# A gated linear-attention kernel with a two-layer head: products and casts moved from GpSimd to VectorE, and a new step table

## The chip, the cores and the metric

The kernel runs on one core of one Trainium2 chip. The metric is the device time of one execution in microseconds (us). Each time below is the median of several executions on the chip. A run that is over 1.5% above the fastest of the same kernel is labelled slow and is left out of the ratios. The chip is not the same for all groups of runs; the kernel before ran beside each group, so kernels of different groups are compared by their ratio to it.

A core has a matrix engine (TensorE, PE in the profile; its weight loads are PEld), a vector engine (VectorE, DVE), an activation engine (ScalarE, ACT), a general engine (GpSimd, POOL) and a small one that here only issues DMAs (SyncE, SP). "SPq" is SyncE's instruction queue. Times in a trace are from the start of the span of that execution.

## The reference

The first half is an mLSTM cell: batch 4, 8 heads, 768 steps, head size 40, in fp32. The second half is a two-layer head with a squareplus between the layers.

```python
for t in range(S):                       # per batch row and head
    m_new  = max(f_gate[t] + m, i_gate[t])
    f_stab = exp(f_gate[t] + m - m_new);  i_stab = exp(i_gate[t] - m_new);  m = m_new
    C = f_stab * C + i_stab * outer(v[t], k[t])
    n = f_stab * n + i_stab * k[t]
    y[t] = sigmoid(o_gate[t]) * (C @ q[t]) / max(abs(n @ q[t]), 1.0)
x = y  as [B*S, H*D]                     # 3072 x 320
h = x @ w_in                             # 320 -> 2048
out = (0.5 * (h + sqrt(h*h + 4))) @ w_out   # 2048 -> 320, fp32
```

The kernel computes the recurrence in a short form for tiles of 128 steps (it checks on the chip that the gates allow this).

## The kernel before

There are 12 blocks: 4 batch rows with 3 pairs of 128-step tiles. For each block, q is cast to bf16 (`qb`), transposed (`qT`), multiplied with the row's state (`np`; for the first tile of a row there are also scores of q and k, `sp`), scaled (`y`), gated (`xt`), and transposed again (`xT`). Then come four groups of hidden units (`hp`, 12 matmuls each; Square and Sqrt on ScalarE; `gt` on VectorE) and the second matmuls (`op`). All engines have hand-made instruction orders. A slot is one hidden group, a step is half a slot, and a table says at which step each piece of attention work of a later block is put into the stream.

```python
STEPS = {   # per block: pr = cast of q, q_ = transpose of q, n0/n1 = scores+y+gate of a tile, x = transpose of x
    ...
    4: dict(pr=16, q_=18, n0=20, n1=23, x=26),
    5: dict(pr=19, k_=19, q_=22, s0=25, s1=26, n0=28, n1=30, x=34),
    ...
}
QDMA = (2, 3, 5, 6, 7, 8, 9, 10, 11)   # blocks whose q is transposed by a DMA
XDMA = (3, 4, 5, 7, 8, 9, 10, 11)      # the same for x
ROWS = (11, 23, 41)                    # steps at which the next batch row's loads are issued
...
        def crossbar(out, in_):
            nc.sync.dma_start(out=out, in_=in_, transpose=True)      # issued by SyncE
...
        def s_num(blk, t, tag, peng=nc.gpsimd):
            ...                                                      # np on TensorE; den, y1 on VectorE
            for lo, o in ((0, xt[blk % 2][:, t, 0:DM]), (DM - 64, xt[blk % 2][:, t, DM:])):
                peng.tensor_tensor(out=o, in0=y[:, lo:DM], in1=s[:, lo:DM], op=ALU.mult)   # the gate product
...
        def load_row(b):                                             # all issued by GpSimd
            chunk(kf, "kf", k, b, nc.gpsimd)                         # 80 KB
            chunk(vf, "vf", v, b, nc.gpsimd)                         # 80 KB
            later(ql, "ql", q, b, 1, NTL, nc.gpsimd)                 # 800 KB
            later(ol, "ol", o_gate, b, 1, NTL, nc.gpsimd)            # 800 KB
            chunk(q0, "q0", q, b, nc.gpsimd)                         # 160 KB
            chunk(o0, "o0", o_gate, b, nc.gpsimd)                    # 160 KB
...
        for n, hs in enumerate(ROWS):
            pre.setdefault(hs, []).append(lambda n=n: load_row(n + 1))
...
                at(pre, 2 * slot)          # casts and loads of this step, on GpSimd
                at(plan, 2 * slot)         # transposes, scores, gates of this step
```

GpSimd works through one list in which gate products, casts and the issue of loads stand in order, and a product in that list waits for VectorE's `y`. SyncE has a second list, in which transposing DMAs and output stores stand in order, and a store waits for its eviction.

Of the kernel before, what the change touches and what calls it, by code (L numbers as in the profile page):

```python
# [8 lines left out]
BF = mybir.dt.bfloat16  # L9
I32 = mybir.dt.int32  # L10
AF = mybir.ActivationFunctionType
ALU = mybir.AluOpType
# [3 lines left out]


STEPS = {
    1: dict(pr=None, q_=1, n0=3, n1=3, x=4),
    2: dict(pr=9, k_=1, q_=11, s0=12, s1=13, n0=13, n1=13, x=15),  # L20
    3: dict(pr=13, g=14, q_=14, n0=16, n1=17, x=18),
    4: dict(pr=16, q_=18, n0=20, n1=23, x=26),
    5: dict(pr=19, k_=19, q_=22, s0=25, s1=26, n0=28, n1=30, x=34),
    6: dict(pr=28, g=33, q_=30, n0=36, n1=34, x=39),
    7: dict(pr=33, q_=38, n0=42, n1=44, x=52),
    8: dict(pr=42, k_=43, q_=45, s0=50, s1=52, n0=53, n1=55, x=60),
    9: dict(pr=52, g=58, q_=53, n0=60, n1=59, x=65),
    10: dict(pr=62, q_=63, n0=68, n1=70, x=71),
    11: dict(pr=68, k_=68, q_=68, s0=73, s1=77, n0=79, n1=80, x=85),
}  # L30
SIGM = (15, 30, 58)
EARLY = (2, 3, 7, 8, 13, 14, 15, 16, 17, 18, 23, 24, 25, 31, 34, 39, 40, 42)
SECOND = (0, 0, 0, 0, 0, 2, 0, 1, 1, 2, 1, 1, 1, 1, 1, 1, 0, 2, 0, 1, 0, 1, 1, 1, 1, 1, 2, 1, 1, 2, 1, 1, 0, 2, 1, 1, 0, 1, 1, 0, 2, 0, 2, 1)
QT = (1, 2, 9, 10, 11)
XT = (3, 5, 7, 11)
OUT = (0, 2, 3, 13, 17, 19, 20, 21, 22)
ALONE = (4, 5, 6, 7, 8, 9, 12, 13, 14, 15, 18, 19, 24, 25, 26, 27, 30, 31, 34, 35, 38, 39, 40, 41, 42, 43)
QDMA = (2, 3, 5, 6, 7, 8, 9, 10, 11)
XDMA = (3, 4, 5, 7, 8, 9, 10, 11)
CLEAR = 8  # L40
ROWS = (11, 23, 41)
FLAGS = (56, 67, 75, 82)


def general_path(tc, q, k, v, i_gate, f_gate, o_gate, out, w_in, w_in3, w_out, ident):
# [144 lines left out]
def kernel(  # L190
# [12 lines left out]
    nc = tc.nc  # L203
    B, H, S, D = q.shape
# [8 lines left out]
    G3 = 3  # L213
# [4 lines left out]
    NU = NF // UF  # L218

    const = ctx.enter_context(tc.tile_pool(name="const", bufs=1))  # L220
    short = ExitStack()
    res = short.enter_context(tc.tile_pool(name="res", bufs=1))
    work = short.enter_context(tc.tile_pool(name="work", bufs=2))
# [13 lines left out]
    with tc.manual_schedule():  # L237
# [80 lines left out]
        for i in range(2):  # L318
            for m in (qb[i][:, 0], qb[i][:, 1]):
# [7 lines left out]
                                     op0=ALU.add, op1=ALU.bypass)  # L327
        nc.vector.tensor_tensor(out=nb[:, 0, :], in0=F[:, 0:T], in1=fi[:, 1, 0:T], op=ALU.subtract)
        nc.vector.tensor_tensor_scan(out=nb[:, 1, :], data0=nb[:, 0, :], data1=nb[:, 0, :], initial=1e30,
                                     op0=ALU.min, op1=ALU.bypass)  # L330
# [7 lines left out]
        state = {}  # L338
# [34 lines left out]
        def qcast(blk, eng, ts=(0, 1)):  # L373
            b = blk // 3
            for t in ts:
                tt = PAIRS[blk % 3][t]
                src = q0[b] if tt == 0 else tile_of(ql, b, tt)
                for o, i in zip(padded(qb[blk % 2][:, t]), heads(src)):
                    eng.tensor_copy(out=o, in_=i)  # L379
# [62 lines left out]
            nc.vector.tensor_tensor(out=state[b, "scm"][:, half * 3:half * 3 + len(hs), :], in0=sp,  # L442
                                    in1=caus.unsqueeze(1).to_broadcast([128, len(hs), 128]), op=ALU.mult)

        def s_num(blk, t, tag, peng=nc.gpsimd):
            b, tt = blk // 3, PAIRS[blk % 3][t]
            np_ = psum([128, H, D + 1], FP, tag, "np")
            if tt == 0:
                for n, h in enumerate((0, 2, 3, 5, 6)):
                    if n % 2:  # L450
                        o, r = np_[:, h:h + 1, :], state[b, "vw"][:, h:h + 1, :]
                    else:
                        o, r = np_[:, h:h + 2, :], vpb[b % 2][:, n // 2, :, :]
                    nc.tensor.matmul(out=o, lhsT=state[b, "scm"][:, n, :], rhs=r, start=True, stop=True)
            else:
                for g in range(G3):
                    n = min(3, H - 3 * g)
                    nc.tensor.matmul(out=np_[:, 3 * g:3 * g + n, :], lhsT=state[blk, "qT"][:, t, g, :],  # L458
                                     rhs=state[b, "gm"][:, 3 * g:3 * g + n, :], start=True, stop=True)
            den = work.tile([128, H, 1], FP, tag="den", name="den", bufs=3)  # L460
            dn = np_[:, :, D:D + 1]
            nc.vector.tensor_reduce(out=den, in_=dn, axis=AX.X, op=ALU.max, apply_absolute_value=True)  # L462
            y1 = work.tile([128, H, D], FP, tag="y1", name="y1", bufs=3)
            if tt == 0:
                nc.vector.tensor_tensor(out=den, in0=den, in1=wE[:, 1, b * H:(b + 1) * H].unsqueeze(2), op=ALU.max)
                nc.vector.reciprocal(out=den, in_=den)
                nc.vector.tensor_tensor(out=y1, in0=np_[:, :, 0:D], in1=den.to_broadcast([128, H, D]), op=ALU.mult)
            else:

                nc.vector.reciprocal(out=den, in_=den)  # L470
                nc.vector.scalar_tensor_tensor(out=y1, in0=den.to_broadcast([128, H, D]), scalar=1.0, in1=np_[:, :, 0:D],  # L471
                                               op0=ALU.min, op1=ALU.mult)
            y, s = (a.rearrange("p h d -> p (h d)") for a in (y1, state[b, "sig"][:, tt]))
            for lo, o in ((0, xt[blk % 2][:, t, 0:DM]), (DM - 64, xt[blk % 2][:, t, DM:])):
                peng.tensor_tensor(out=o, in0=y[:, lo:DM], in1=s[:, lo:DM], op=ALU.mult)  # L475

        def s_x(blk, tag):
            if blk in XDMA:
                xT = work.tile([128, 2, G3, 128], BF, tag="xT", name="xT", bufs=3)
                crossbar(xT.rearrange("p t g n -> p (t g) n"), xt[blk % 2].rearrange("p t n -> p (t n)"))  # L480
                state[blk, "xT"] = xT
                return
            xp = psum([128, 2, G3, 128], BF, tag, "xp")
            for t in range(2):
                for g in range(G3):
                    nc.tensor.transpose(xp[:, t, g, :], xt[blk % 2][:, t, g * 128:(g + 1) * 128], ident)
            xT = work.tile([128, 2, G3, 128], BF, tag="xT", name="xT", bufs=3)
            evacuate(XT, blk, xT, xp)
            state[blk, "xT"] = xT
# [3 lines left out]
        def idle(n):  # L493

            for _ in range(n):
                nc.tensor.matmul(out=warm[:, 0:128], lhsT=ident, rhs=ident, start=True, stop=True)  # L496
# [11 lines left out]

        for o, i in zip(padded(qb[0][:, 1]), heads(tile_of(ql, 0, 2))):
            nc.scalar.activation(out=o, in_=i, func=AF.Copy)  # L510
        idle(8)
        tp = [psum([128, 384], BF, "hp", "tp") for t in range(2)]
        np_ = psum([128, 2 * H, 64], FP, "hp", "np")
        qT = work.tile([128, 2, G3, 128], BF, tag="qT", name="qT")
        for t in range(2):
            for g in range(G3):
                nc.tensor.transpose(tp[t][:, g * 128:(g + 1) * 128], qb[0][:, t, g, :], ident)
        nc.vector.tensor_copy(out=qT[:, 0], in_=tp[0].rearrange("p (g n) -> p g n", g=G3))
        nc.scalar.activation(out=qT[:, 1], in_=tp[1].rearrange("p (g n) -> p g n", g=G3), func=AF.Copy)
        sigm(0, 1, 3)  # L520
        idle(4)
        for t in range(2):
            for g in range(G3):
                n = min(3, H - 3 * g)
                nc.tensor.matmul(out=np_[:, t * H + 3 * g:t * H + 3 * g + n, 0:D + 1], lhsT=qT[:, t, g, :], rhs=state[0, "gm"][:, 3 * g:3 * g + n, :],
                                 start=True, stop=True)
        den = const.tile([128, 2 * H, 1], FP, name="den0")
        y1 = const.tile([128, 2, H, D], FP, name="y0")
# [3 lines left out]
                                       in1=np_[:, :, 0:D], op0=ALU.min, op1=ALU.mult)  # L532
# [65 lines left out]
        def put_pre(hs, blk):  # L598
            b = blk // 3
            todo = pre.setdefault(hs, [])  # L600
            if blk % 3 == 2 and b:
                todo.append(lambda: khcast(b, nc.gpsimd))
            if blk % 3 == 0:
                todo.append(lambda: kcast(b, nc.gpsimd))
                todo.append(lambda: vcast(b, nc.gpsimd))
            todo.append(lambda: qcast(blk, nc.gpsimd))

        def put_block(blk, pr, q_, n0, n1, x, g=None, k_=None, s0=None, s1=None):
            b = blk // 3
# [18 lines left out]
        for n, hs in enumerate(ROWS):  # L628
            pre.setdefault(hs, []).append(lambda n=n: load_row(n + 1))
        for b, hs in enumerate(SIGM):  # L630
            put(hs, sigm, b + 1, 0, NTL)
        early.update(EARLY)
        for hs, f in zip(FLAGS, (flag1, flag2, flag3, flag4)):
            put(hs, f)
# [75 lines left out]
        def unit(blk, u):  # L710

            hp = hps.pop((blk, u))
            t1 = moe.tile([128, UF, 256], FP, tag="t1", name="t1")
            nc.scalar.activation(out=t1, in_=hp, func=AF.Square, scale=0.5)  # L714
            nc.scalar.activation(out=t1, in_=t1, func=AF.Sqrt, bias=1.0)  # L715
            return lambda: nc.vector.scalar_tensor_tensor(out=gts[blk][:, u * UF:(u + 1) * UF, :], in0=hp, scalar=0.5, in1=t1,  # L716
                                                          op0=ALU.mult, op1=ALU.add)

        todo = list(range(NBLK * NU - NU))
# [22 lines left out]
        blk = NBLK - 1  # L742
# [60 lines left out]
```

## Time and profile before

| | before |
|---|---|
| time, median of 3 runs | 155.05 us (154.83 to 156.91) |
| span of the profiled execution | 152.4 us |
| mean granted TensorE clock in it | 0.995 |
| busy us of PE, DVE, ACT, POOL | 132.8, 100.8, 121.7, 77.4 |

### The profile page before, as it was taken

The numbers are of one execution on the slowest core, as the hardware profiler recorded it, in microseconds if no ns is written. First come the engines' busy times: TensorE is split into PE (matmuls) and PEld (weight loads), VectorE is DVE, ScalarE is ACT, GpSimd is POOL, SyncE is SP. The second block draws the span as 40 slices with busy tenths as digits, with TensorE's granted clock in tenths as the row PEclk, the third lists the DMA queues.
The fourth block names the chain that finished last, engine by engine and source line by source line (L and its number), as shares of the span: only waits on it lengthen the run. The fifth ranks groups of instructions, "written<-read, shape, count | busy, mean of one in ns | idle before, by whom it ended". The sixth has DMA issues, their size and how long they took to land.

```text
span 152.4 us, 3186 instructions
## 1 busy us (share of the span) xinstructions
PE 132.8 (87%) x1185; PEld 93.3 (61%) x1185; DVE 100.8 (66%) x190; ACT 121.7 (80%) x130; POOL 77.4 (51%) x168
## 2 busy tenths in 40 slices
PE   6697679747999995899999899899999999999970
PEld 5684446435578673667775677666677676666740
DVE  4764556666778678388787689775799794765410
ACT  3648959938999779999997568999979989699610
POOL 7998889975363997337969014448022050000000
PEclk9999999999999999999999999999999999999997
DMA  2999999999037699503799150132333103101111
GB/s 49 253 239 197 191 211 210 282 301 124 34 78 120 138 342 227 143 28 84 225 308 162 68 149 4 43 95 54 101 103 84 60 31 95 43 6 41 71 65 49
DMA packets 29140, 19.45 MB, mean 128 GB/s; under 512 B 20752, under 2 KB 27200, under 8 KB 29120
## 3 DMA queue, kind: packets, MB, share of 16 engines
q0 software_dynamic: 5824, 10.49, 29.6%
q1 hardware_dynamic: 22240, 8.55, 26.3%
q10 hardware_dynamic: 1056, 0.16, 0.7%
q8 instruction: 10, 0.16, 0.4%
q14 instruction: 10, 0.08, 0.2%
HBM read 13.96 MB, written 3.93 MB: 117 GB/s over the span
## 4 chain that ended last, share of the span: by engine, by line
PE 52%; DVE 16%; DMA 10%; ACT 8%; POOL 5%; issue 4%; SPq 0%; DVEq 0%; POOLq 0%; ACTq 0%
PE op L668 24%; PE hp L695 16%; PE hp L702 5%; DVE gt L716 5%; ACT t L714 5%; DMA xT<-xt 4%; DMA qT<-qb 3%; ACT t L715 3%; POOL xt L475 2%; PE np L458 2%; DVE y L471 2%; PE warm L496 2%; DVE osb L396 2%; DMA fi<-in_i_gate_dram 1%; DMA out_dram<-osb 1%
## 5 line engine op out<-in xcount | busy, mean ns | idle before, releaser
L716 DVE SCALAR_TENSOR_TENSOR gt<-hp,t 128x1024 bf16<-128x1024 f32 x48 | 58.1, 1220 | 16.0 <-ACT t L715 16.0
L714 ACT ACTIVATE t<-hp 128x1024 f32<-128x1024 f32 x48 | 48.7, 1014 | 14.4 <-PE hp L702 7.0
L668 PE MATMUL op<-w_out,gt 128*128 128x320 bf16 x384 | 57.6, 299 | 0.9 <-DVE osb L396 0.7
L695 PE MATMUL hp<-xT,w_in 128*128 128x256 bf16 x384 | 49.8, 273 | 3.6 <-DMA xT<-xt 1.7
L715 ACT ACTIVATE t<-t 128x1024 f32<-128x1024 f32 x48 | 50.7, 1057 | 1.5
L475 POOL TENSOR_TENSOR xt<-y,sig 128x320 bf16<-128x320 f32 (+1 forms) x44 | 25.1, 592 | 44.8 <-DVE y L471 24.3
L668 PEld LDWEIGHTS <-gt 128*128 128x128 bf16 x384 | 35.6, 98 | 15.9 <-issue 3.7
L695 PEld LDWEIGHTS <-w_in 128*128 128x128 bf16 x384 | 35.9, 98 | 11.2 <-issue 4.1
L702 PE MATMUL hp<-xT,w_in 64*128 64x256 bf16 x192 | 18.0, 274 | 0.0
L396 DVE COPY osb<-op 128x320 f32<-128x320 f32 x15 | 7.3, 486 | 9.6 <-PE op L668 6.3
L702 PEld LDWEIGHTS <-w_in 64*128 64x128 bf16 x192 | 6.0, 94 | 9.2 <-issue 8.8
L471 DVE SCALAR_TENSOR_TENSOR y<-den,np 128x320 f32<-128x320 f32 x18 | 8.8, 488 | 1.6
L379 POOL CAST qb<-ql 128x240 bf16<-128x240 f32 (+1 forms) x32 | 9.0, 316 | 0.5 <-DMA ql<-in_q_dram 0.5
L496 PE MATMUL warm<-ident 128*128 128x128 bf16 x68 | 7.8, 297 | 1.4 <-POOL identF L269 1.4
L458 PE MATMUL np<-gm,qT 128*128 128x123 bf16 (+1 forms) x54 | 5.7, 214 | 2.8 <-DVE y L471 1.1
L496 PEld LDWEIGHTS <-ident 128*128 128x128 bf16 x68 | 6.7, 140 | 1.5 <-POOL identF L269 1.4
L390 ACT ACTIVATE sig<-ol 128x1600 f32<-128x1600 f32 (+2 forms) x5 | 6.3, 1260 | 1.4 <-DMA ol<-in_o_gate_dram 1.4
L458 PEld LDWEIGHTS <-qT 128*128 128x128 bf16 x54 | 3.8, 98 | 5.6 <-issue 2.6
L442 DVE TENSOR_TENSOR scm<-sp,caus 128x384 bf16<-128x384 f32 (+1 forms) x8 | 3.9, 488 | 3.6 <-PE sp L438 3.6
L462 DVE TENSOR_REDUCE den<-np 128x8 f32<-128x8 f32 x22 | 3.5, 160 | 3.3 <-PE np L458 2.3
L394 ACT ACTIVATE osb<-op 128x320 f32<-128x320 f32 x9 | 3.8, 424 | 1.9 <-PE op L668 1.9
L248 POOL DMA_DIRECT2D ql<-in_q_dram x5 | 4.5, 907 | 0.5 <-DMA w_in<-in_moe_w_in_dram 0.5
(103 smaller groups left out, 102.0 us busy)
## 6 DMA issues: line engine op xcount, KB each, us to landing
out_dram<-osb SPq DMA_DIRECT2D x24, 160.0 KB, 1.8
ql<-in_q_dram POOLq DMA_DIRECT2D x3, 800.0 KB, 6.1
ol<-in_o_gate_dram POOLq DMA_DIRECT2D x3, 800.0 KB, 7.7
w_out<-in_moe_w_out_dram POOLq DMA_DIRECT2D x2, 640.0 KB, 11.1
o<-in_o_gate_dram POOLq DMA_DIRECT2D x4, 160.0 KB, 7.7
q<-in_q_dram POOLq DMA_DIRECT2D x4, 160.0 KB, 8.4
w_in<-in_moe_w_in_dram POOLq DMA_DIRECT2D x2, 256.0 KB, 5.6
w_in<-in_moe_w_in_dram POOLq DMA_DIRECT2D x1, 512.0 KB, 8.2
```

The source lines that it names most:

```text
L379: eng.tensor_copy(out=o, in_=i)
L396: nc.vector.tensor_copy(out=dst, in_=src)
L458: nc.tensor.matmul(out=np_[:, 3 * g:3 * g + n, :], lhsT=state[blk, "qT"][:, t, g, :], rhs=state[b, "gm"][:, 3 * g:3 * g + n, :], start=Tru ...
L471: nc.vector.scalar_tensor_tensor(out=y1, in0=den.to_broadcast([128, H, D]), scalar=1.0, in1=np_[:, :, 0:D], op0=ALU.min, op1=ALU.mult)
L475: peng.tensor_tensor(out=o, in0=y[:, lo:DM], in1=s[:, lo:DM], op=ALU.mult)
L496: nc.tensor.matmul(out=warm[:, 0:128], lhsT=ident, rhs=ident, start=True, stop=True)
L668: nc.tensor.matmul(out=op, lhsT=gts[blk][:, ff, ts * 128:(ts + 1) * 128], rhs=w_out[:, ff, :], start=(ff == 0), stop=(ff == NF - 1))
L695: nc.tensor.matmul(out=hps[blk, u][:, f, :], lhsT=w_in[:, g, ff * 128:(ff + 1) * 128], rhs=xT[:, :, g, :], start=start and g == 0 and f % ...
L702: nc.tensor.matmul(out=hps[blk, u][:, 2 * i + f, :], lhsT=w_in3[p, (2 * u + f) * 128:(2 * u + f + 1) * 128], rhs=xT[p, :, 2, :], start=sta ...
L714: nc.scalar.activation(out=t1, in_=hp, func=AF.Square, scale=0.5)
L715: nc.scalar.activation(out=t1, in_=t1, func=AF.Sqrt, bias=1.0)
L716: return lambda: nc.vector.scalar_tensor_tensor(out=gts[blk][:, u * UF:(u + 1) * UF, :], in0=hp, scalar=0.5, in1=t1, op0=ALU.mult, op1=ALU ...
```

## The change

VectorE takes seven gate products (`XV`) and block 4's q casts (`QV`) from GpSimd. ScalarE takes five more output evictions and gives up one qT eviction. The chain ahead of the first matmuls becomes shorter, and all steps are placed anew. The list for squares on VectorE (`SQD`) is there, but empty. The diff, cut to its core:

```diff
 STEPS = {
-    4: dict(pr=16, q_=18, n0=20, n1=23, x=26),
-    5: dict(pr=19, k_=19, q_=22, s0=25, s1=26, n0=28, n1=30, x=34),
+    4: dict(pr=16, q_=19, n0=20, n1=23, x=29),
+    5: dict(pr=19, k_=19, q_=20, s0=25, s1=27, n0=29, n1=31, x=34),
     ...                                      # all other rows, SIGM, EARLY, SECOND, FLAGS also differ
-QT = (1, 2, 9, 10, 11)
+QT = (2, 6, 7, 8, 10, 11)
-OUT = (0, 2, 3, 13, 17, 19, 20, 21, 22)
+OUT = (0, 6, 8, 10, 13, 14, 15, 16, 17, 18, 19, 20, 21, 22)
+SQD = ()
+XV = (3, 4, 5, 8, 9, 12, 16)                 # tile = 2 * block + t: 8 and 9 are block 4
+QV = (4,)
-ROWS = (11, 23, 41)
+ROWS = (11, 24, 41)
...
+            peng = nc.vector if blk * 2 + t in XV else nc.gpsimd
             for lo, o in ((0, xt[blk % 2][:, t, 0:DM]), (DM - 64, xt[blk % 2][:, t, DM:])):
                 peng.tensor_tensor(out=o, in0=y[:, lo:DM], in1=s[:, lo:DM], op=ALU.mult)
...
-        idle(8)
+        idle(2)
...
-            todo.append(lambda: qcast(blk, nc.gpsimd))
+            todo.append(lambda: qcast(blk, nc.vector if blk in QV else nc.gpsimd))
```

More of the change, by code (lines that the diff above doesn't have):

```diff
@@ L18 @@
 STEPS = {
-    1: dict(pr=None, q_=1, n0=3, n1=3, x=4),
-    2: dict(pr=9, k_=1, q_=11, s0=12, s1=13, n0=13, n1=13, x=15),
-    3: dict(pr=13, g=14, q_=14, n0=16, n1=17, x=18),
-    4: dict(pr=16, q_=18, n0=20, n1=23, x=26),
-    5: dict(pr=19, k_=19, q_=22, s0=25, s1=26, n0=28, n1=30, x=34),
-    6: dict(pr=28, g=33, q_=30, n0=36, n1=34, x=39),
-    7: dict(pr=33, q_=38, n0=42, n1=44, x=52),
-    8: dict(pr=42, k_=43, q_=45, s0=50, s1=52, n0=53, n1=55, x=60),
-    9: dict(pr=52, g=58, q_=53, n0=60, n1=59, x=65),
@@ L28 @@
-    10: dict(pr=62, q_=63, n0=68, n1=70, x=71),
-    11: dict(pr=68, k_=68, q_=68, s0=73, s1=77, n0=79, n1=80, x=85),
-}
-SIGM = (15, 30, 58)
-EARLY = (2, 3, 7, 8, 13, 14, 15, 16, 17, 18, 23, 24, 25, 31, 34, 39, 40, 42)
-SECOND = (0, 0, 0, 0, 0, 2, 0, 1, 1, 2, 1, 1, 1, 1, 1, 1, 0, 2, 0, 1, 0, 1, 1, 1, 1, 1, 2, 1, 1, 2, 1, 1, 0, 2, 1, 1, 0, 1, 1, 0, 2, 0, 2, 1)
-QT = (1, 2, 9, 10, 11)
-XT = (3, 5, 7, 11)
-OUT = (0, 2, 3, 13, 17, 19, 20, 21, 22)
-ALONE = (4, 5, 6, 7, 8, 9, 12, 13, 14, 15, 18, 19, 24, 25, 26, 27, 30, 31, 34, 35, 38, 39, 40, 41, 42, 43)
+    1: dict(pr=None, q_=1, n0=2, n1=3, x=7),
@@ new lines @@
+    2: dict(pr=10, k_=2, q_=11, s0=12, s1=12, n0=13, n1=12, x=15),
+    3: dict(pr=14, g=14, q_=15, n0=17, n1=16, x=18),
+    4: dict(pr=16, q_=19, n0=20, n1=23, x=29),
+    5: dict(pr=19, k_=19, q_=20, s0=25, s1=27, n0=29, n1=31, x=34),
+    6: dict(pr=28, g=33, q_=32, n0=36, n1=34, x=39),
+    7: dict(pr=34, q_=35, n0=41, n1=43, x=50),
+    8: dict(pr=40, k_=44, q_=44, s0=50, s1=51, n0=52, n1=54, x=59),
+    9: dict(pr=44, g=58, q_=49, n0=60, n1=61, x=62),
+    10: dict(pr=63, q_=67, n0=69, n1=71, x=72),
@@ L38 @@
+    11: dict(pr=68, k_=70, q_=69, s0=73, s1=75, n0=79, n1=80, x=84),
+}
+SIGM = (15, 30, 59)
+EARLY = (3, 4, 7, 8, 12, 15, 17, 18, 19, 22, 25, 26, 39)
+SECOND = (0, 0, 0, 0, 0, 2, 1, 1, 1, 1, 1, 1, 1, 1, 0, 2, 1, 1, 0, 1, 1, 1, 0, 1, 1, 1, 1, 1, 2, 2, 2, 0, 0, 2, 1, 1, 0, 1, 1, 0, 2, 0, 2, 1)
+QT = (2, 6, 7, 8, 10, 11)
+XT = (7, 8, 9)
+OUT = (0, 6, 8, 10, 13, 14, 15, 16, 17, 18, 19, 20, 21, 22)
+ALONE = (4, 5, 6, 7, 8, 9, 12, 13, 16, 17, 18, 19, 20, 21, 26, 27, 30, 31, 40, 41, 42, 43)
 QDMA = (2, 3, 5, 6, 7, 8, 9, 10, 11)
@@ L39 @@
 XDMA = (3, 4, 5, 7, 8, 9, 10, 11)
+SQD = ()
+XV = (3, 4, 5, 8, 9, 12, 16)
+QV = (4,)
 CLEAR = 8
-ROWS = (11, 23, 41)
-FLAGS = (56, 67, 75, 82)
+ROWS = (11, 24, 41)
+FLAGS = (57, 62, 79, 85)
 def general_path(tc, q, k, v, i_gate, f_gate, o_gate, out, w_in, w_in3, w_out, ident):
@@ L443, in s_sc, with s_num @@
                                     in1=caus.unsqueeze(1).to_broadcast([128, len(hs), 128]), op=ALU.mult)
-        def s_num(blk, t, tag, peng=nc.gpsimd):
+        def s_num(blk, t, tag):
             b, tt = blk // 3, PAIRS[blk % 3][t]
@@ L483, in s_x @@
             xp = psum([128, 2, G3, 128], BF, tag, "xp")
-            for t in range(2):
-                for g in range(G3):
+            for g in range(G3):
+                for t in range(2):
                     nc.tensor.transpose(xp[:, t, g, :], xt[blk % 2][:, t, g * 128:(g + 1) * 128], ident)
@@ L510 @@
             nc.scalar.activation(out=o, in_=i, func=AF.Copy)
-        idle(8)
+        idle(2)
         tp = [psum([128, 384], BF, "hp", "tp") for t in range(2)]
         np_ = psum([128, 2 * H, 64], FP, "hp", "np")
-        qT = work.tile([128, 2, G3, 128], BF, tag="qT", name="qT")
+        qT = [const.tile([128, G3, 128], BF, name=f"qT0{t}") for t in range(2)]
         for t in range(2):
@@ L517 @@
                 nc.tensor.transpose(tp[t][:, g * 128:(g + 1) * 128], qb[0][:, t, g, :], ident)
-        nc.vector.tensor_copy(out=qT[:, 0], in_=tp[0].rearrange("p (g n) -> p g n", g=G3))
-        nc.scalar.activation(out=qT[:, 1], in_=tp[1].rearrange("p (g n) -> p g n", g=G3), func=AF.Copy)
+        nc.vector.tensor_copy(out=qT[0], in_=tp[0].rearrange("p (g n) -> p g n", g=G3))
+        nc.scalar.activation(out=qT[1], in_=tp[1].rearrange("p (g n) -> p g n", g=G3), func=AF.Copy)
         sigm(0, 1, 3)
@@ L524 @@
                 n = min(3, H - 3 * g)
-                nc.tensor.matmul(out=np_[:, t * H + 3 * g:t * H + 3 * g + n, 0:D + 1], lhsT=qT[:, t, g, :], rhs=state[0, "gm"][:, 3 * g:3 * g + n, :],
+                nc.tensor.matmul(out=np_[:, t * H + 3 * g:t * H + 3 * g + n, 0:D + 1], lhsT=qT[t][:, g, :], rhs=state[0, "gm"][:, 3 * g:3 * g + n, :],
                                  start=True, stop=True)
@@ L713, in unit @@
             t1 = moe.tile([128, UF, 256], FP, tag="t1", name="t1")
-            nc.scalar.activation(out=t1, in_=hp, func=AF.Square, scale=0.5)
+            if blk * NU + u in SQD:
+                nc.vector.scalar_tensor_tensor(out=t1, in0=hp, scalar=0.25, in1=hp, op0=ALU.mult, op1=ALU.mult)
+            else:
+                nc.scalar.activation(out=t1, in_=hp, func=AF.Square, scale=0.5)
             nc.scalar.activation(out=t1, in_=t1, func=AF.Sqrt, bias=1.0)
```

## The prediction

> **What bounds the kernel now.** I read the page first, then TensorE by stretches, then its waits, then the chain of waits, then the timelines around each wait. The page, busy time and slices:
>
> ```profile
> PE 132.8 (87%) x1185; PEld 93.3 (61%) x1185; DVE 100.8 (66%) x190; ACT 121.7 (80%) x130; POOL 77.4 (51%) x168
> ...
> PE   6697679747999995899999899899999999999970
> ...
> ACT  3648959938999779999997568999979989699610
> ```
>
> TensorE is the fullest engine, so a gain has to come out of its 19.6 us of idle time (152.4 - 132.8). The slices say where: the first ten (to 38 us), one at 57 to 61 us, and the tail. The stretches put numbers on it (columns: length, then busy us of PE, PEld, DVE, ACT, POOL, then clock, DMA share, GB/s):
>
> ```profile
> 28.00:32.00 4.00, 2.33 (x23) 1.49 (x21) 2.62 (x4) 3.62 (x5) 3.94 (x11) 1.00 0.93 310
> 32.00:36.00 4.00, 2.63 (x30) 1.75 (x28) 2.55 (x8) 1.25 (x2) 2.47 (x6) 1.00 1.43 260
> ...
> 57.00:62.00 5.00, 3.31 (x32) 2.06 (x29) 3.99 (x7) 4.60 (x6) 4.06 (x12) 1.00 1.13 247
> 62.00:70.00 8.00, 7.15 (x68) 4.95 (x67) 5.36 (x11) 7.91 (x9) 1.89 (x5) 1.00 0.29 72
> 70.00:80.00 10.00, 10.00 (x94) 7.42 (x93) 7.76 (x13) 9.84 (x11) 8.74 (x18) 1.00 0.71 210
> 80.00:90.00 10.00, 9.22 (x82) 6.44 (x81) 6.96 (x11) 7.11 (x7) 3.47 (x11) 1.00 0.78 127
> ```
>
> Summed over all stretches, PE idles 3.4 us before 12.87 (start-up), 7.0 from there to 40, only 4.3 from 40 to 145.3, and 4.9 in the tail. From 100 to 145 it is busy all but 0.2 us: the later half offers nothing. From 62 to 80 ScalarE too is full (17.75 of 18 us). TensorE's own waits name the causes:
>
> ```profile
> PE hp L695 <- DMA xT<-xt: 1.7, 1, 1.7
> ...
> PE sp L438 <- DVE scm L442: 1.2, 1, 1.2
> ...
> PE np L458 <- DVE y L471: 1.1, 1, 1.1
> ...
> PE np L454 <- DVE y L471: 1.0, 1, 1.0
> ...
> PE sp L438 <- DMA qT<-qb: 0.8, 1, 0.8
> PE op L668 <- DVE osb L396: 0.7, 1, 0.7
> ```
>
> And the chain of waits shows the 1.7 us one from its source:
>
> ```profile
> 48.08 1.15 POOL xt L475 x2
> 49.23 0.67 POOL kf L243
> ...
> 53.25 0.87 POOL o L243
> 54.14 1.14 POOL xt L475 x2
> 55.30 5.72 DMA xT<-xt
> 61.07 1.05 PE hp L695 x8
> ```
>
> GpSimd sits for 5 us in issuing the next row's loads, so block 4's second gate product starts at 54.14 although VectorE finished its input at 50.3; the transposing DMA then takes 5.72 us, and TensorE stands.
>
> **What the Trainium skill says.** "GPSIMD Engine Reference", section 4.1 Engine selection, puts two-input elementwise work on GpSimd at about twice VectorE's time. The trace says 1.7: a gate product is 864 + 320 = 1184 ns on GpSimd; VectorE's two of 128x640 and 128x128 took 825 and 288 ns, a slope of 537/512 = 1.05 ns an element, so my estimate for 320 and 64 elements is 489 + 221 = 710 ns. "PSUM — Partial Sum Buffer", section The four PSUM rules, keeps GpSimd off PSUM, so only products and casts between SBUF tiles can leave GpSimd, and PSUM evictions move between VectorE and ScalarE alone; the diff does just that. "DMA: Bandwidth & Descriptors", section Issuing engines are not separate DMA queues, says that DMAs of all engines interleave on the same 16 engines; the trace agrees: an xT transpose lands in 2.5 us as median and in 5.72 when row loads are in flight.
>
> **The change part by part.**
> Lists first, because some do nothing: the list for squares on VectorE is empty, so no square moves, and the xT eviction list names only blocks that go by DMA. What moves: seven gate products and block 4's two q casts from GpSimd to VectorE; block 1's qT eviction from ScalarE to VectorE; nine output evictions on ScalarE become fourteen.
> - VectorE: 7 x 0.71 = +5.0; two casts of 0.384 + 0.486 = +1.7; qT +0.55; five evictions of 0.486 = -2.4. Net +4.8, to 105.6 us of 152: not a bound on average.
> - GpSimd: 7 x 1.18 + 2 x (0.382 + 0.250) = -9.6. It isn't the bound; only blocking counts.
> - ScalarE: 5 x 0.424 - 0.79 = +1.3, to 123.0.
> - TensorE: six warm-up matmuls fewer; two more pairs of hidden-layer groups (the single list goes from 26 to 22 of 40). A pair's eight half-height matmuls took 0.54 us against 2 x 0.33, so 2 x 0.11 = -0.2 us.
>
> *Start.* The eight warm-ups took 0.85 us in the chain; two take 0.21, but the q cast on VectorE ends at 7.15 where transposes began at 7.39. Gain about 0.25 us, and the first hidden matmul at about 12.6 instead of 12.87.
>
> *12.9 to 28 us.* The order comparison shows block 1's two score products (np) back to back: their steps 2 and 3 fall in different PSUM banks, where 3 and 3 shared one. That removes the 1.1 us wait; the fourth hidden group moves ahead of the xT transposes; ScalarE loses the 0.79 us qT eviction. Walking the new order with durations of the old trace, group 5's square comes some 1.5 us earlier (about 23.7 instead of 25.16). But the second output matmul set needs the second half of w_out, which landed at 27.1 (issue at 15.0 plus 12.1), and its issue is paced by the loads before it, which don't change. It started at 27.15 after a wait of 0.2. I expect that wait to grow to about 1.5 us: **both the 0.25 us and this 1.5 us are lost there.**
>
> *28 to 37.4 us.* Block 2's score chain is serial through one bank: scm, sp, scm, np, y, np, y, with TensorE idle for 3.0 of the 8 us from 28 to 36. The new order puts a set of eight output matmuls (1.09 us in the chain) inside it, which in the old order came after. Gain **1.1 us**. The other waits of the chain stay.
>
> *40 to 62 us.* Block 4's products go to VectorE right behind y, so its xT leaves near 51 instead of 55.3, and even 5.7 us of flight ends before about 59, when it is wanted. The 1.7 us wait goes. But ScalarE was busy 4.60 of 5 us in that stretch and stays full to 80, with two or so extra evictions (0.4 each). TensorE can't run three buffers ahead of it. I count half: **0.9 us**.
>
> *80 to 100 us.* Block 8's q cast is placed two steps earlier, its transpose one step earlier, and no store waiting for VectorE stands just ahead of it on SyncE's queue: the 0.8 us wait on qT goes, and ScalarE has slack here. **0.8 us**. Of the 0.7 us osb wait and smaller ones I count **0.4**.
>
> Sum: 1.1 + 0.9 + 0.8 + 0.4 + 0.2 = 3.4 us. A whole new placement brings new waits too; I charge 0.4. Net 3.0: 155.05 - 3.0 = 152.0 us, 1.9% less.
>
> **Rivals.**
> *ScalarE is the bound.* For it: full from 40 to 50 and from 62 to 80, and it gets 1.3 us more. Then lost TensorE waits come back as waits for hidden-layer buffers, and only the early 1.1 and part of the 0.8 remain: 153 to 154.5. Against it: over the span it has 30 us free, and the late half is TensorE's.
> *VectorE's order becomes the wait.* Products now stand between its evictions (0.71 us each, ahead of a 1.22 us gt that frees a buffer). For it: ScalarE already waits 5.4 us for gt. Then 154 to 156. Against it: VectorE has 47 us free, and only seven products move.
> *The early stretch gains more.* If w_out lands earlier, or TensorE fills the wait, another 1 to 1.5 us comes, and with all of the 40 to 100 us waits gone: 149.5 to 150.5. Against it: load order and issuing engine are unchanged, and the loads kept the DMA queues full to 28 us.
>
> **Range and chances.** The terms carry from 1 us (ScalarE rival) to 5 us (everything gained), so 149.8 to 154.3, with 152.0 in the middle. Two per cent is 3.1 us, just beyond my net 3.0, so faster and same are nearly even; slower needs the second rival to cost more than all gains.
>
> **What would show it.** Right: VectorE near 105.6, GpSimd near 68, ScalarE near 123 us busy; first hidden matmul near 12.6; the wait of op for w_out near 1.5 us; TensorE idle from 40 to 100 falling from about 4 to about 2 us; no xT wait near 60. Wrong: w_out landing well before 27 us; TensorE waits for gt in 60 to 80 as long as the xT wait that went; a new wait over 1 us anywhere after 40.

## More of the kernel before

One view is added here, the timeline of GpSimd and SyncE around 50 us. The columns are start in us, duration in us, engine, line, operation, output<-input, and in brackets the idle time before it and who ended it. For a DMA issue, the duration is that of the issue, not of the transfer.

```profile
46.88 1.62 SPq L400 DMA_TRANSPOSE qT<-qb  x1
48.08 1.15 POOL L475 TENSOR_TENSOR xt<-y,sig 128x320 bf16<-128x320 f32 x2 [3.55 <-DVE y L471]
49.17 0.73 POOL L243 DMA_DIRECT2D kf<-in_k_dram  x1
...
50.58 0.91 POOL L248 DMA_DIRECT2D ql<-in_q_dram  x1
51.48 0.90 POOL L248 DMA_DIRECT2D ol<-in_o_gate_dram  x1
...
55.30 1.28 SPq L400 DMA_TRANSPOSE xT<-xt  x1
```

SyncE issues the transposing DMA for block 5's q at 46.88. GpSimd stands for 3.55 us until VectorE has block 4's first `y`, then does the gate product. Block 4's x follows at 55.30.

## The result

The changed kernel took 162.76 us as a median of 4 runs (161.58 to 164.46, the highest labelled slow). The kernel before, on the same chip, took 155.74 us (154.83 to 156.91). The ratio is 1.042, with a 95% interval of 1.030 to 1.055: **slower**, and outside the predicted range. Here and below, a ratio is the mean time of one kernel's fast runs over that of the other's of the same rounds, so it isn't quite the ratio of the medians.

The page of the changed kernel, busy time and slices of 4.03 us:

```profile
span 161.3 us, 3158 instructions
...
PE 134.8 (84%) x1179; PEld 94.3 (58%) x1179; DVE 104.5 (65%) x204; ACT 122.3 (76%) x134; POOL 68.8 (43%) x150
...
PE   5795788688996009999699999989999999999980
...
PEclk9999999999999855899999999999999999999999
```

The engine totals are close to those predicted (VectorE 104.5 against 105.6, GpSimd 68.8 against 68, ScalarE 122.3 against 123.0). What is new is a hole: two slices from 52 us in which TensorE does nothing, with half clock in the second of them and in the one behind it. The stretches around it (columns as in the prediction: length, busy us of PE, PEld, DVE, ACT, POOL, then clock, DMA share, GB/s):

```profile
45.00:50.00 5.00, 5.00 (x46) 3.69 (x45) 4.76 (x12) 4.55 (x6) 5.00 (x9) 1.00 0.91 229
50.00:55.00 5.00, 0.83 (x7) 0.38 (x4) 1.09 (x3) 1.72 (x2) 1.48 (x6) 1.00 1.25 149
55.00:60.00 5.00, 0.00 (x0) 0.00 (x0) 0.00 (x0) 0.00 (x0) 0.21 (x2) 0.56 0.66 151
60.00:65.00 5.00, 4.47 (x22) 2.48 (x23) 2.82 (x3) 1.67 (x2) 0.00 (x0) 0.50 0.09 31
```

From 55 to 60 us PE, DVE and ACT do nothing at all and GpSimd nearly nothing; only DMAs move, at 151 GB/s. TensorE's own waits name the one that it stands for, ahead of the ones that the prediction spoke of:

```profile
PE sp L441 <- DMA qT<-qb: 9.7, 1, 9.7
...
PE hp L699 <- DVE gt L723: 1.3, 1, 1.3
```

The 1.7 us wait for the xT that goes by DMA is gone, but that proves nothing: here this xT left only at 66.45, after the stall. In its place stands a wait of 9.7 us for block 5's transposed q, which had been no wait of note before. The timeline shows how it came about:

```profile
43.95 0.73 POOL L246 DMA_DIRECT2D kf<-in_k_dram  x1
...
45.35 0.91 POOL L251 DMA_DIRECT2D ql<-in_q_dram  x1
...
46.26 0.90 POOL L251 DMA_DIRECT2D ol<-in_o_gate_dram  x1
46.35 1.36 SPq L403 DMA_TRANSPOSE qT<-qb  x1
...
47.37 0.63 DVE L479 TENSOR_TENSOR xt<-y,sig 128x320 bf16<-128x320 f32 x2
```

The transposing DMA leaves at nearly the same time as before (46.35 against 46.88). The loads, though, leave 5.2 us earlier: 43.95 against 49.17. Block 4's gate products now run on VectorE (at 47.37), so GpSimd no longer waits for `y` ahead of the loads. In the step table the loads moved from 23 to 24, which is later; on the chip they went earlier. Before, the transpose was 3.7 us ahead of the first 800 KB load. Now it is 1.0 us behind it. The view of DMA issues from 43 to 62 us shows what that does (columns: KB each, us from issue to landing). First the kernel before, with the landing of block 5's qT from its view of that tile, then the changed kernel:

```profile
ql<-in_q_dram POOLq DMA_DIRECT2D x1, 800.0 KB, 6.1
ol<-in_o_gate_dram POOLq DMA_DIRECT2D x1, 800.0 KB, 7.7
...
DMA to landing us min/median/max: 3.2/3.2/3.2
```

```profile
ql<-in_q_dram POOLq DMA_DIRECT2D x1, 800.0 KB, 8.6
ol<-in_o_gate_dram POOLq DMA_DIRECT2D x1, 800.0 KB, 15.5
...
qT<-qb SPq DMA_TRANSPOSE x1, 14.0
```

The transpose took 14.0 us instead of 3.2, the second large load 15.5 instead of 7.7. Below, such a pair of slow transfers is called a crawl. Not every overlap of a transpose with loads is one, as the experiments will show.

The clock makes it worse. The trace's clock records show half speed from 55.6 to 65.8 us. TensorE stopped at 50.8 and restarted at 60.5, so 5.2 us of work ran at half speed: eight `hp` matmuls took 1.71 us in the chain where they took 1.05 before. The Trainium skill, "TensorE: Matmul & The Clock Gate", section What's actually happening, gives two states, half and full, set by activity in free-running windows of 3413 ns. The trace agrees: 10.24 us of half clock are three such windows, and the clock fell 4.8 us after the stop and came back 5.3 us after the restart.

So the lost time is 9.7 us of standing and, as an estimate from the 5.2 us of work, about 5.2/2 = 2.6 us of half clock, some 12.3 us. The net loss between the two profiled spans is 161.3 - 152.4 = 8.9 us, so the rest of the change must have gained something. The experiments test both halves of this.

### The profile page after: what moved, and what is told of

The parts are those of the page before. It is cut to its first block, busy times and chain, and to the rows that moved or that the text cites. A ratio compares the mean times of both kernels' runs of the same rounds, so it can differ in the third digit from the quotient of the medians.

```text
span 161.3 us, 3158 instructions
## 1 busy us (share of the span) xinstructions
PE 134.8 (84%) x1179; PEld 94.3 (58%) x1179; DVE 104.5 (65%) x204; ACT 122.3 (76%) x134; POOL 68.8 (43%) x150
## 3 DMA queue, kind: packets, MB, share of 16 engines
q1 hardware_dynamic: 22240, 8.55, 26.3%
## 4 chain that ended last, share of the span: by engine, by line
PE 47%; DMA 20%; DVE 9%; ACT 8%; POOL 7%; issue 5%; SPq 1%; POOLq 0%; DVEq 0%; ACTq 0%
PE op L672 23%; PE hp L699 16%; DMA qT<-qb 9%; DMA w_out<-in_moe_w_out_dram 7%; PE hp L706 5%; DVE gt L723 4%; DMA w_in<-in_moe_w_in_dram 4%; ACT t L721 3%; ACT t L722 2%; ACT sig L393 1%; PE sp L441 1%; DVE osb L399 1%; PE np L461 1%; POOL xt L479 1%; ACT L390 1%
## 5 line engine op out<-in xcount | busy, mean ns | idle before, releaser
L672 PE MATMUL op<-w_out,gt 128*128 128x320 bf16 x384 | 59.0, 303 | 1.8 <-DMA w_out<-in_moe_w_out_dram 0.8
L699 PE MATMUL hp<-xT,w_in 128*128 128x256 bf16 x384 | 50.9, 276 | 4.0 <-DVE xT L399 1.7
L672 PEld LDWEIGHTS <-gt 128*128 128x128 bf16 x384 | 36.1, 98 | 18.0 <-issue 4.6
L699 PEld LDWEIGHTS <-w_in 128*128 128x128 bf16 x384 | 35.9, 99 | 12.2 <-issue 6.2
L479 POOL TENSOR_TENSOR xt<-y,sig 128x320 bf16<-128x320 f32 (+1 forms) x30 | 17.4, 603 | 57.8 <-DVE y L474 30.7
L441 PE MATMUL sp<-qT,kT 128*128 128x128 bf16 x20 | 2.7, 240 | 10.4 <-DMA qT<-qb 9.7
L399 DVE COPY osb<-op 128x320 f32<-128x320 f32 x10 | 4.9, 486 | 8.9 <-PE op L672 8.9
L382 POOL CAST qb<-ql 128x240 bf16<-128x240 f32 (+1 forms) x28 | 7.9, 320 | 4.9 <-issue 3.5
L441 PEld LDWEIGHTS <-kT 128*128 128x128 bf16 x20 | 1.8, 106 | 11.6 <-issue 11.1
L397 ACT ACTIVATE osb<-op 128x320 f32<-128x320 f32 x14 | 5.9, 424 | 2.0 <-PE op L672 1.9
```

Of the source, the lines that this page charges most:

```text
L382: eng.tensor_copy(out=o, in_=i)
L672: nc.tensor.matmul(out=op, lhsT=gts[blk][:, ff, ts * 128:(ts + 1) * 128], rhs=w_out[:, ff, :], start=(ff == 0), stop=(ff == NF - 1))
L699: nc.tensor.matmul(out=hps[blk, u][:, f, :], lhsT=w_in[:, g, ff * 128:(ff + 1) * 128], rhs=xT[:, :, g, :], start=start and g == 0 and f % ...
```

## The experiments

Theory A: the freed GpSimd issues the row's loads earlier, so block 5's transposing DMA falls among them, and a transposing DMA and large loads in flight together slow each other. Rivals: the transpose is slow because of its own new place in the table or its reader; any added traffic at that place does the same; the loads as such are too early, whatever is beside them. The kernel before ran in the same rounds as each of them: 155.52 us beside e1 to e4, 155.30 beside e5 to e7 and v1, 155.47 beside e8, v2 and v3, and 155.24 beside e9. All of these kernels gave correct results.

| kernel | us | ratio to before, 95% |
|---|---|---|
| after, loads held to block 4's second product (e1) | 156.11 | 1.003 (0.994 to 1.011) |
| after, block 4's products back on GpSimd (e2) | 155.75 | 0.999 (0.991 to 1.007) |
| before, only block 4's products on VectorE (e3) | 169.43 | 1.086 (1.076 to 1.096) |
| after, block 5's q transposed by TensorE (e4) | 152.75 | 0.981 (0.973 to 0.988) |
| e4 + the transposing DMA into unread memory (e5) | 157.51 | 1.014 (1.007 to 1.022) |
| e4 + a plain copy of that size there (e6) | 152.46 | 0.982 (0.977 to 0.987) |
| after, loads held to block 4's first product (e7) | 151.92 | 0.974 (0.968 to 0.980) |
| e7, block 4's x sent earlier (e8) | 153.53 | 0.986 (0.980 to 0.992) |
| e8, loads 0.9 us later (e9) | 160.29 | 1.025 (1.014 to 1.035) |
| e4 with three more table entries (v1) | 155.24 | 0.998 (0.993 to 1.003) |
| v1 without one of them (v2) | 152.85 | 0.984 (0.979 to 0.988) |
| e7, block 4's x transposed by TensorE (v3) | 152.87 | 0.983 (0.978 to 0.988) |

### The cause taken back: e1 and e2

```diff
 # e1, on after: GpSimd copies one element of block 4's second gated tile ahead of the loads
+        held = const.tile([1, 1], BF, name="held")
+        pre.setdefault(ROWS[1], []).append(lambda: nc.gpsimd.tensor_copy(out=held, in_=xt[0][0:1, 1, 0:1]))
 # e2, on after
-XV = (3, 4, 5, 8, 9, 12, 16)
+XV = (3, 4, 5, 12, 16)
```

> The changed kernel with one GpSimd copy of one element of block 4's second gated tile put ahead of the third row's loads (the second of the three later load bursts), so that GpSimd can't issue them before VectorE has made that tile. Theory A (the loads went out at 44 to 49 us because their engine lost the gate products that had held it, and met the q transpose issued at 46.35): the loads start near 51, the q transpose of block 5 lands in 3 to 6 us instead of 14.0, TensorE's 9.7 us wait goes, and the time falls from 162.8 to between 150.5 and 154. Rival B (the transpose is slow because of its own new place behind the kT transpose, the small v copy and a store): the loads move, the 14 us and 162 us stay. Rival C (only some of the slowness is the loads'): 155 to 160.

> The changed kernel with only block 4's two gate products put back on GpSimd, where they stand ahead of the third row's loads. Theory A: loads start near 51 to 52, the q transpose of block 5 lands in 3 to 6 us, time 151 to 155, a little over the run that only holds the loads, since block 4's transposed tile is late again as in the kernel before. Rival B: the 14 us transpose and about 162 us stay.

Both put the loads back behind block 4's products (first load at 50.84 and 50.73), and in both the 9.7 us wait is gone and most of the lost time is back. So it was the time of the loads, not the engine that multiplies: e1 leaves the products on VectorE. The times missed the expected ranges by 2.1 us (e1) and 0.8 us (e2), because the stall didn't vanish but moved. TensorE's waits in e1:

```profile
PE hp L701 <- DMA xT<-xt: 4.5, 1, 4.5
```

The hold was too long. Block 4's x now left 2.1 us behind the first large load and took 8.3 us. In both kernels 6.83 us of half clock followed this wait (from 61.1 and 61.2 us), so the wait cost more than its own 4.5 us.

### The cause alone: e3

```diff
 # on before
+            peng = nc.vector if blk == 4 else peng
```

> The kernel before with one part of the change alone: block 4's two gate products on VectorE, all steps as they were. Theory A: GpSimd reaches the loads near 44.5 instead of 49.2, just ahead of block 5's q transpose (46.9 before), which then takes 10 us or more to land; time 160 to 166 against 155.7. Rival B (the new placement, not the product's engine): no slow transpose, 154 to 156.5.

This one line in the kernel before costs more than the whole change: 169.43 us. The loads went out at 45.71, the q transpose 1.0 us behind the first large one, and it took 17.4 us. TensorE's waits:

```profile
PE sp L438 <- DMA qT<-qb: 13.3, 2, 12.8
```

Since nothing else of the new placement is in this kernel, the new step table isn't needed for the stall. The time lies above the expected 160 to 166 us: 13.65 us of half clock came with the stall (from 58.0 us). The profiled execution also has 3.41 us of half clock from 34.2 us, before the loads, so about 1 us of the profile's loss isn't the collision's (block 5's q left 1.2 us later than before).

### The victim taken away: e4, e5 and e6

```diff
 # e4, on after
-QDMA = (2, 3, 5, 6, 7, 8, 9, 10, 11)
+QDMA = (2, 3, 6, 7, 8, 9, 10, 11)
 # e5, on e4
+            if blk == 5:
+                scr = const.tile([128, 2 * G3, 128], BF, name="scr")
+                crossbar(scr, qb[1].rearrange("p t g n -> p (t g n)"))
 # e6, on e5: the same bytes, not transposed
-                scr = const.tile([128, 2 * G3, 128], BF, name="scr")
-                crossbar(scr, qb[1].rearrange("p t g n -> p (t g n)"))
+                scr = const.tile([128, 2 * G3, 160], BF, name="scr")
+                nc.sync.dma_start(out=scr[:, :, 0:128], in_=qb[1].rearrange("p t g n -> p (t g) n"))
```

> The changed kernel with block 5's q transposed by TensorE and evicted by VectorE, so no transposing DMA is issued while the early loads are in flight. Theory A (the two kinds of transfer slow each other): the loads still start at 44, but the large ones land in 6 to 9 us instead of 8.6 and 15.5; no 9.7 us wait; time 151 to 155. Rival D (the loads are slow at this moment whatever else runs): the loads still need 15 us and later users (third row's gates and casts) wait; time above 156.

> The run with block 5's q transposed by TensorE (152.75 us), plus the same transposing DMA of the same tile at the same place of SyncE's queue, into a scratch tile that nobody reads. Theory A (a transposing DMA issued about 1 us behind the first large load slows both, whoever reads it): the two large loads land in 8 to 9.5 and 15 to 16 us again, the scratch transpose in about 14, though TensorE has no need of it; the time rises by 1 to 6 us only by what waits for the loads and for later transposes of the same queue. Rival E (TensorE's stop itself prolonged the transfers, or the waiting consumer made it slow): loads land in 5.6 and 8.3 us as without it, time within 0.7 us of 152.75.

> As the run before, but the scratch transfer is a plain copy of the same 192 KB from SBUF to SBUF in runs of 256 bytes, on the same queue at the same place. If the transposing is what clashes: loads in 5.5 to 6.5 and 8 to 9.5 us, time 152.5 to 154. If any transfer of so many small packets beside the loads does it: loads near 9 and 15 us as with the transpose.

In e4 the loads leave as early as in after (43.67), and the two large ones land in 5.6 and 8.3 us. So early loads alone do no harm, and without the one transposing DMA the kernel runs in 152.75 us. In e5 that DMA is back, into memory that nobody reads. Its issues from 43 to 66 us:

```profile
ol<-in_o_gate_dram POOLq DMA_DIRECT2D x1, 800.0 KB, 14.8
...
scr<-qb SPq DMA_TRANSPOSE x1, 16.4
```

The crawl is there without a reader, so no reader causes it. It costs 5.1 us against e6, which ran in the same rounds, through a later 3.3 us wait for xT and half clock behind it. The plain copy in e6 landed in 9.7 us, the large loads in 6.0 and 9.8 (the second a little above the 8 to 9.5 us expected), and the time was that of e4. **It is the transposing, not the added bytes.** Nor is it the number of packets: against e4 the transpose adds 800 to the profile's count (22240 against 21440), the copy 784 (22224). e6 differs from e5 also in the pattern of its writes, so a plain copy in other runs of bytes isn't covered.

### The change without the collision: e7

```diff
 # on after: as e1, but the first gated tile
+        held = const.tile([1, 1], BF, name="held")
+        pre.setdefault(ROWS[1], []).append(lambda: nc.gpsimd.tensor_copy(out=held, in_=xt[0][0:1, 0, 0:1]))
```

> The changed kernel with the loads held only until block 4's first gated tile, so the large load goes out near 49.4, some 3 us behind block 5's q transpose (46.3) and some 5 us ahead of block 4's transposed tile (54.4). Theory A with order and distance mattering: the q transpose lands in 3 to 5 us, the loads in 5.6 to 7 and 7.5 to 9; block 4's tile takes 5 to 6 us and costs 0.5 to 2.5 us of waiting against 4.5 with the long hold; time 152.5 to 155. If any overlap at all clashes: 158 or more.

GpSimd and SyncE in e7's timeline:

```profile
46.25 1.53 SPq L403 DMA_TRANSPOSE qT<-qb  x1
...
49.36 0.91 POOL L251 DMA_DIRECT2D ql<-in_q_dram  x1
49.46 5.21 SPq L655 DMA_DIRECT2D out_dram<-osb  x2
...
54.72 1.28 SPq L403 DMA_TRANSPOSE xT<-xt  x1
```

The q transpose is 3.1 us ahead of the first large load again and lands in 3.1 us. This is the fastest kernel measured: 151.92 us, just under the expected 152.5 to 155, and 2.6% under before by the ratio, with an interval that reaches across 2% and overlaps with those of e4, e6, e8, v2 and v3. It is the change as it was meant. That it lies where the prediction put the change (152.0) is partly luck, as shown below. What is left is a 2.2 us wait for xT: SyncE stood from 49.46 to 54.67 in output stores, so block 4's x left at 54.72, although its second product was done at 51.2.

### How near is too near: e8 and e9

```diff
 # e8, on e7
-    4: dict(pr=16, q_=19, n0=20, n1=23, x=29),
+    4: dict(pr=16, q_=19, n0=20, n1=23, x=24),
 # e9, on e8: two memsets on GpSimd ahead of the loads
+        fill = const.tile([128, 2, 480], BF, name="fill")
+        for i in range(2):
+            pre[ROWS[1]].append(lambda i=i: nc.gpsimd.memset(fill[:, i], 0.0))
```

> The short-hold run (151.92 us) with block 4's xT transpose five steps earlier in the order, so one store no longer stands between block 4's gated tile (about 51) and its transpose; it should go out near 51 instead of 54.7, which is 1 to 2 us behind the first large load (49.4) as in the two slow kernels. If nearness behind the large loads' issue is what matters: the transpose takes 10 us or more, the second large load lands in 13 to 16 us, and the time is 156 to 162 although the transpose leaves earlier. If an earlier transpose is simply better: it lands near 57, the 2.2 us wait goes, 149.5 to 151.5.

> The run before (block 4's transpose early, 153.53 us, transpose 1.86 us behind the first large load, 9.4 us of flight, loads undisturbed at 6.6 and 8.2) with two GpSimd fills of about 0.9 us together ahead of the loads, so that the same transpose is about 1 us behind the same load, as in the three runs with crawling transfers (0.93 to 1.00 us). If the distance decides: the second large load lands in 13 to 16 us, the transpose in 12 to 17, and the time is 156 to 163. If not (something else of the first three, such as the kT transpose, the small v copy and a store just ahead of it, is needed): loads near 6.6 and 8.2 us, transpose 8 to 10, time 152.5 to 155.

e8 was meant to gain the 2.2 us, and didn't. Its x left 2.3 us earlier (52.44, 1.9 us behind the first large load) but took 9.4 us instead of 6.0, and so landed at 61.8, 0.4 us behind the last of the loads. TensorE still waited 2.1 us for it, and 3.41 us of half clock followed (from 63.3 us), which e7 doesn't have. Neither a crawl nor a gain, so it missed both expectations. About 1 us of e8's profiled span comes from another half-clock stretch near 16 to 19 us, before the edit acts. e9 does the same with both a little nearer, because its hold shifts the loads by two memsets:

```profile
50.22 0.91 POOL L251 DMA_DIRECT2D ql<-in_q_dram  x1
51.00 1.23 SPq L403 DMA_TRANSPOSE xT<-xt  x1
51.12 0.90 POOL L251 DMA_DIRECT2D ol<-in_o_gate_dram  x1
```

Now x leaves 0.8 us behind the first large load. TensorE's timeline shows what became of it:

```profile
68.33 1.86 PE L704 MATMUL hp<-xT,w_in 128*128 128x256 bf16 x8 [9.96 <-DMA xT<-xt]
```

The transpose took 17.3 us, the second large load 15.6, and the time was 160.29 us. So the stall can be made again with another transpose (of x, not of q) at another place, by 1.1 us of distance. e9's profiled run is labelled slow; its two fast runs, 157.94 and 160.05 us, say the same against 153.53 for e8. The pairs around block 4 and 5, and one that is in every kernel (block 2's q beside the second row's loads), sorted by the distance from the issue of the first large load to that of the transposing DMA:

| kernel, transpose | distance, us | transpose took, us | first and second large load took, us |
|---|---|---|---|
| before, qT of block 5 | -3.7 (ahead) | 3.2 | 6.1, 7.7 |
| e7, qT of block 5 | -3.1 (ahead) | 3.1 | 6.6, 8.2 |
| all 14 kernels, qT of block 2 | -1.3 (ahead) | 4.8 to 5.5 | 5.8 to 7.4, 7.9 to 10.3 |
| e9, xT of block 4 | 0.8 | 17.3 | 7.8, 15.6 |
| e5, unread | 0.9 | 16.4 | 6.6, 14.8 |
| after, qT of block 5 | 1.0 | 14.0 | 8.6, 15.5 |
| e3, qT of block 5 | 1.0 | 17.4 | 9.3, 15.7 |
| e8, xT of block 4 | 1.9 | 9.4 | 6.6, 8.2 |
| e1, xT of block 4 | 2.1 | 8.3 | 5.8, 7.6 |
| e2, xT of block 4 | 2.2 | 8.3 | 5.8, 7.6 |
| before, xT of block 4 | 4.7 | 5.7 | 6.1, 7.7 |
| e7, xT of block 4 | 5.4 | 6.0 | 6.6, 8.2 |

Other pairs are left out, among them the later transposes that were issued while another one crawled (3.6 to 13.7 us in e3, e5 and e9).

So overlap alone is not enough. From 1.9 us on, the loads keep their time, and the transpose lands 0.4 to 0.9 us after the last of them. Between 0.8 and 1.0 us, transpose and second load crawl. Ahead of the first load, even by only 1.3 us, nothing crawls: block 2's q is in flight together with the first large load for 3.5 us or more in every kernel. Nothing was measured between -1.3 and 0.8 us or between 1.0 and 1.9 us. What in the DMA engines makes the difference wasn't shown. In every crawling case the transpose was issued behind the first large load, and before or within 0.1 us after the second; where it came behind both without a crawl, it was at least 0.9 us behind the second. So distance and order are not told apart, and the large loads were never separated from the four small ones issued with them. That stays open.

### Other versions: v1, v2 and v3

```diff
 # v1, on e4; v2 is v1 without the SECOND part
-    5: dict(pr=19, k_=19, q_=20, s0=25, s1=27, n0=29, n1=31, x=34),
-    6: dict(pr=28, g=33, q_=32, n0=36, n1=34, x=39),
+    5: dict(pr=19, k_=19, q_=22, s0=25, s1=27, n0=29, n1=31, x=34),
+    6: dict(pr=28, g=33, q_=30, n0=36, n1=34, x=39),
-SECOND = (0, 0, 0, 0, 0, 2, 1, 1, ...)
+SECOND = (0, 0, 0, 0, 0, 1, 2, 1, ...)
 # v3, on e7
-XDMA = (3, 4, 5, 7, 8, 9, 10, 11)
+XDMA = (3, 5, 7, 8, 9, 10, 11)
```

> An attempt at a better version: the run with block 5's q on TensorE, with that transpose two steps later (it waited 1.4 us for its PSUM bank), block 6's q transpose two steps earlier (1.0 us wait), and the second half of the first output tile after the seventh hidden group instead of before it (1.5 us wait for w_out). If these waits were worth their size, 150 to 151.5 us; if they were slack, or come back elsewhere, 152 to 153.5.

> The combined attempt without its third part: block 5's q on TensorE with that transpose two steps later, and block 6's q transpose two steps earlier; the first output tile as in the change. If moving half of the first output tile was what cost (it left TensorE idle before block 2's scores, and the granted clock fell to 0.5 after it): 150.5 to 152.5, no 0.5 clock slice near 36 us. If one of the two steps did: 154 to 156.

> The short-hold run with block 4's xT made by TensorE and VectorE (0.5 and 0.55 us of work) instead of the transposing DMA that waited behind the loads and cost TensorE 2.2 us. If that wait was on the path: 150 to 151.3. If ScalarE, full from 60 on, sets the pace there: no gain, 151.5 to 152.5.

None beat e7. v1, expected at 150 to 153.5, lost 2.5 us to e4: with one set of output matmuls moved a slot later, TensorE waited 2.2 us for another qT near 29 us, and a stretch of half clock followed. v2, without that part, is level with e4, so the two steps of q gain nothing. v3 takes e7's xT wait away, and is no faster. Its profiled execution is already 1.6 us behind e7 at 44 us, before the edit acts, after a half-clock stretch from 16 to 19.4 us; it is 1.4 us behind at the end. In between, v3 caught up about 1.2 us and lost it again: new waits of 0.65 us (for the new xT eviction) and 0.98 us (for a qT) took the place of the 2.2 us. So taking this wait away gained almost nothing.

## Why the prediction was wrong

**The totals and the early stretch held.** The first hidden matmul came at 12.23 us in after, against about 12.6 predicted. The wait for w_out grew from 0.2 to 0.8 us in after, 1.0 in e7 and 1.5 in e4, against 1.5 predicted. TensorE's busy time from 28 to 37.4 us rose from 5.72 to 7.21 us in e7, 1.5 us against the 1.1 counted, of which 0.55 was lost between 12.6 and 28 us. Counted by hidden matmuls, e7 is 0.9 us ahead of before after a quarter of them (near 49 us). The gate product, estimated at 0.71 us on VectorE, took 0.63.

**80 to 100 us held.** TensorE was busy 18.55 of 20 us before and 19.57 in e7, so 1.0 us against 0.8 + 0.4, and the wait for block 8's qT is gone. (These are fixed stretches of time, and e7 runs ahead by then, so they don't hold exactly the same work.)

**The step that failed is "40 to 62 us".** It said that block 4's xT "leaves near 51 instead of 55.3", and that "the 1.7 us wait goes". Two things in it are wrong.

- It moved the products and left the loads where they were. The chain of waits that it quoted has block 4's product at 48.08 and the first load at 49.23, back to back: the product was what held the loads. With the product gone, they went out 5.2 us earlier, into block 5's transposing DMA. The rival on early gains even says "load order and issuing engine are unchanged", which is true, and misses that the time of issue isn't. The line on GpSimd, "It isn't the bound; only blocking counts", was right, but blocking was counted only as a loss. Here it was the thing that kept two transfers apart. e3 shows this step alone: it costs 8.6%.
- xT doesn't leave near 51 either. Where the loads are held (e1, e7), it left at 54.4 and 54.7, because SyncE's list has an output store ahead of it that waits for an eviction (e7: VectorE's copy at 53.84), and because the new table itself moves block 4's x from step 26 to 29. In the changed kernel itself it left at 66.45. The step looked at when the data is ready, not at the list of the engine that issues the transfer. And when e8 sent it at 52.4, the loads made it land no earlier. So the 0.9 us counted for this stretch wasn't there even without the collision: from 50 to 62 us TensorE was busy 9.74 us in e7 and 10.31 before, and its 1.7 us wait for xT became 2.2 us. From 40 to 100 us it was idle for 3.4 us in e7 and 4.1 before, where the prediction expected about 2.

**No rival had it.** In e7, which has the same table and the same products on VectorE, neither ScalarE nor VectorE's order takes the gain away, and TensorE's busy time from 100 to 145 us is the same as before (44.80 and 44.79). The prediction's list of what would make it wrong did name "a new wait over 1 us anywhere after 40", and that is what came, nine times as long. It also counted no clock loss behind a long wait, which was about 2.6 us here.

**The loss adds up.** After and e7 have the same tables, so they can be compared matmul by matmul (the hidden ones, `hp`). After is 0.1 us behind just before the stall and 12.2 us behind it, which is the 9.7 us wait and the 2.6 us of half clock. Then e7's own wait for xT brings the difference to 9.8 us, and a wait of 1.3 us for `gt` (at 79 us in after), which e7 doesn't have, brings it to 11.3 us. The profiled spans differ by 161.3 - 150.1 = 11.2 us.

**Partly luck: e7's 152.0.** Between the profiled spans, e7 gains 152.4 - 150.1 = 2.3 us, not 3.0. The gain between the medians of its rounds is larger, 155.30 - 151.92 = 3.4 us. The kernel before had mean clocks of 0.978 to 0.988 in these rounds, against 0.995 in its profile, and e7's fast runs 0.992 to 0.996. That the clock makes up the rest is likely, but no run shows it.

## What to carry to other kernels

Before work is taken off an engine that also issues transfers, ask what stands behind that work in its list, when it will now go out, and which transfers it will meet. That two transfers overlap doesn't say that they will crawl: here a transpose 1.3 us ahead of the loads did no harm, and one 0.8 to 1.0 us behind the first did. A wait that looks like a loss may be what spaces two transfers, and it is better to make such a spacing explicit: one element copied on the issuing engine turned 162.8 us into 151.9 (ratios to before of 1.042 and 0.974). For a transfer's start, read the list of the engine that issues it, not only the time its data is ready.

## What the Trainium skill lacked or had wrong

- "DMA: Bandwidth & Descriptors", Rules for kernel authors, says that a transpose next to ordinary DMAs needs nothing. The results were correct in all 12 kernels of the experiments, so for correctness no run contradicts it. It lacks the cost: beside two 800 KB loads, the first issued 0.8 to 1.0 us before it, one transposing DMA of 192 KB took 14.0 to 17.4 us instead of the 3.1 of e7, and the second load 14.8 to 15.7 us instead of 7.6 to 8.3. Issued 1.3 us ahead of such loads, it took 4.8 to 5.5 us. A plain copy of the same 192 KB at the same place (e6) left the loads at 6.0 and 9.8 us and cost no time.
- "DMA: Bandwidth & Descriptors", Queues, rings and completion order, says that each DMA engine takes turns between the queues at packet granularity. No run here tests that directly. It lacks what it means for a transpose: issued 1.9 to 5.4 us behind the first large load, it landed only 0.4 to 0.9 us after the last load (5.7 to 9.4 us in flight, against 3.1 in e7, where it went ahead of the large loads), while the second large loads kept their 7.6 to 8.2 us.
